# Attention's PSUM banks lent to the activation's u in steps 8 to 21, and VectorE's operations reordered there

## The chip, the core and the metric

The kernel runs on one core of one Trainium2 chip. The metric is the device time of one execution in microseconds (us). Five engines run side by side, each in its own program order, and wait for one another by semaphores: TensorE (PE in the rows; PEld is its weight load), VectorE (DVE), ScalarE (ACT), GpSimd (POOL) and SyncE (SP), which issues the DMAs. SBUF is the working memory. PSUM holds eight banks of 512 float32 words in each of 128 partitions; TensorE writes its products there.

## What is computed

A retention layer without softmax, and a feed-forward layer with a rational activation on its output:

```python
scores = scale * np.matmul(q, k.transpose(0, 1, 3, 2))      # q, k, v: 8 x 8 x 576 x 64
ret = scores * Dmat[None, :, :, :]                          # gamma_h ** (i - j) for i >= j, else 0
attn = np.matmul(ret, v)
x = attn.transpose(0, 2, 1, 3).reshape(B * S, H * D)        # 4608 x 512
h = x @ w_in                                                # 512 x 2048
P = a[0] + a[1] * h + a[2] * h**2 + a[3] * h**3
Q = 1.0 + np.abs(b[0]) * np.abs(h) + np.abs(b[1]) * h**2
out = (P / (Q + 1e-06)) @ w_out                             # 2048 x 512
```

## The kernel before, in words

Tokens are taken in nine blocks (b) of 512, the 2048 hidden columns in 16 chunks (f) of 128. One step is one pair (b, f). The plan `steps` (line 384) begins with chunks 0 to 7 of block 0 (steps 0 to 7), then has all 16 chunks of block 1 (steps 8 to 23), then chunks 8 to 15 of block 0 (steps 24 to 31), then blocks 2 to 8. 144 steps in all.

Every factor of a product is split in a high and a low part, and three products stand for one. `gemm1` (L282) makes h of a step with 12 matmuls of 512 columns into one of two PSUM banks (`ps_h`); `gemm2` (L347) adds the finished g of an earlier step to the block's sums with 12 more (four banks, `ps_acc`). Two banks (`ps_at`) belong to attention. That is all of PSUM.

Between the two lies the activation, on tiles u, v, p of 128 x 512 float32 in SBUF (u and v in two buffers, p in three):

- `ffn_p` (L293): ScalarE p = a3\*h + a2, then u = |h|; VectorE p = p\*h.
- `ffn_p2` (L303): VectorE p = (p + a1)\*h, the last reader of h.
- `ffn_v` (L307): ScalarE v = |b1|\*u + |b0|; VectorE v = v\*u.
- `ffn_r` (L313), one step later: ScalarE u = Ln(v), then u = Exp(-u), which is the reciprocal of the denominator.
- `ffn_q` (L319), one step later: VectorE p = (p + a0)\*u, v = (v + QC)\*u, p = (v - 2)\*p. The prediction calls these q1, q2, q3.
- `ffn_hi` (L335) and `ffn_lo` (L339), two steps later: ScalarE g's high part from p, then g's low part, on GpSimd for the first 24 steps and on VectorE after.

The weights arrive as 64-bit floats in 64-bit words and are taken apart on the way, one weight tile a step in steps 5 to 23, in `split_weight` (L139), a generator that `split_start` begins and `split_step(j)` moves on: `start` has ScalarE's copy of c, `split0`, `split1` and `split2` one VectorE operation each on c (split1 and split2 also read the words), `split3` ScalarE's high part of w and GpSimd's low part. The tile that one step starts gets its split0 in that step and split1 to split3 in the next.

Attention is done in units of 128 tokens, `scores` to `keep_lo`, in steps that `SCORES` (L50) lists: 1, 3 and 5, then 23, 25 and so on. In steps 8 to 21 none is at work; the scores of a unit are read for the last time in the step after.

The order of the work on each engine is the order in which the names stand in a list: `FIRST` (L34) for steps 0 to 23, `DENSE` and `REST` for later ones; `run` (L411) calls them in that order and leaves out those with nothing to do. `lag` (L387) says how many steps `gemm2` comes after `gemm1`: 4 in steps 8 to 21, otherwise 3 in this part, so step 22 runs two. After each step SP issues up to two loads of weights (`load_weights`). In steps 8 to 21 `FIRST` gives VectorE this order, with i the step:

```
split1, p*h (i), split2, p2 (i), split0, q1, q2, q3 (i-1), v*u (i)
```

The engine operations are all recorded at line 63, the wrapper that keeps program order, so the rows are told apart by their tiles: c<-bits is split1 or split2, TENSOR_SCALAR c<-c is split0, w<-c is split3.

Of the kernel before, what the change touches and what calls it, by code (L numbers as in the profile page):

```python
# [12 lines left out]
F32 = mybir.dt.float32  # L13
# [8 lines left out]
P = 128  # L22
# [7 lines left out]
NF = DFF // P  # L30
# [2 lines left out]
BEFORE = "split1 start scale_q scale_v scores decay outputs split2 add fade keep_hi keep_lo split3 split0".split()  # L33
FIRST = (  # L34
    "split1 gemm1 outputs ffn_p split2 ffn_hi keep_hi ffn_lo gemm2 ffn_r scale_q split3 add fade keep_lo start ffn_p2"
    " scale_v scores decay split0 ffn_q ffn_v"
).split()
DENSE = (
    "gemm1 outputs keep_hi split1 add fade keep_lo ffn_p split2 split0 ffn_v scale_q ffn_hi ffn_r ffn_lo scale_v gemm2"
    " ffn_p2 scores decay split3 ffn_q"  # L40
).split()
REST = (
    "gemm1 ffn_p outputs keep_hi add fade keep_lo ffn_hi ffn_p2 ffn_lo scores decay scale_q scale_v ffn_v gemm2 ffn_r ffn_q"
).split()
END = "ffn_r ffn_hi gemm2 ffn_lo ffn_q".split()

STARTS_BEFORE = [0, 1, 1, 2, 2]
STARTS = [1, 1, 2, 1, 2] + [1] * 19
# [1 line left out]
SCORES = [1, 3, 5, 23, 25, 27, 29, *range(2 * NF, (NB - 1) * NF, 4)]  # L50
# [16 lines left out]
def retention_ffn(ctx: ExitStack, tc: tile.TileContext, qkv, w_in, w_out, ab, masks, gq, gv, out):  # L67
# [20 lines left out]
    ps_at = ctx.enter_context(tc.tile_pool(name="ps_at", bufs=1, space=PSUM))  # L88
# [187 lines left out]
    els = {}  # L276
    gs = {}
    accs = {}
    part = []
    spare = {}  # L280

# [11 lines left out]
    def ffn_p(b, f):  # L293

        h = hs[b, f]
        u, v, p = els[b, f] = [
            (el3 if t == "p" else el).tile([P, 512], F32, tag=t, name=f"{t}{b}_{f}") for t in "uvp"
        ]
        act.activation(p, h, AF.Identity, bias=a2, scale=a3)
        act.activation(u, h, AF.Abs)  # L300
        dve.tensor_tensor(p, p, h, ALU.mult)
# [2 lines left out]
        p = els[b, f][2]  # L304
        dve.scalar_tensor_tensor(p, p, a1, hs.pop((b, f)), ALU.add, ALU.mult)

    def ffn_v(b, f):  # L307

        u, v, p = els[b, f]
        act.activation(v, u, AF.Identity, bias=b0, scale=b1)  # L310
        dve.tensor_tensor(v, v, u, ALU.mult)

    def ffn_r(b, f):  # L313
# [5 lines left out]
    def ffn_q(b, f):  # L319

        u, v, p = els[b, f]
        dve.scalar_tensor_tensor(p, p, a0, u, ALU.add, ALU.mult)
        dve.scalar_tensor_tensor(v, v, QC, u, ALU.add, ALU.mult)
        dve.scalar_tensor_tensor(p, v, 2.0, p, ALU.subtract, ALU.mult)

    def place(b, f):
# [54 lines left out]
    half = NF // 2  # L381
    first = half + NF
    runs = [(0, 0, half), (1, 0, NF), (0, half, NF)] + [(b, 0, NF) for b in range(2, NB)]
    steps = [(b, f, f == r0, f == r1 - 1) for b, r0, r1 in runs for f in range(r0, r1)]
    at = {s[:2]: i for i, s in enumerate(steps)}

    def lag(i):  # L387

        return 4 if NF // 2 <= i < first - 2 or i >= len(steps) - 8 else 3
# [6 lines left out]
    def load_weights(n):  # L396
        for k in [k for _, k in zip(range(n), loads)]:
            load_weight(k)
# [12 lines left out]
    def run(names, todo):  # L411
        todo |= {f"split{j}": (split_step, j) for j in range(4)}
        for name in names:
            if name in todo:
                todo[name][0](*todo[name][1:])
# [43 lines left out]
    for i in range(len(steps) + lag(len(steps))):  # L459
        this, prev, prev2 = (steps[j][:2] if 0 <= j < len(steps) else None for j in (i, i - 1, i - 2))  # L460
        todo = {"gemm2": (products, i), "start": (split_start, STARTS[i] if i < first else 0)}

        out_n = None
        if due and this:
            out_n = due.pop()
            todo |= {f.__name__: (f, out_n) for f in (keep_hi, add, keep_lo, fade)}
            todo["outputs"] = (put_out, out_n)
        if i in SCORES:
            todo |= {f.__name__: (f, nxt) for f in (scores, decay)}
            due.append(nxt)  # L470
            nxt += 1
        if i + 1 in SCORES:
            todo |= {f.__name__: (f, nxt) for f in (scale_q, scale_v)}
        if this:
            todo |= {f.__name__: (f, *this) for f in (gemm1, ffn_p, ffn_p2, ffn_v)}
        if prev:
            todo |= {f.__name__: (f, *prev) for f in (ffn_r, ffn_q)}
        if prev2:
            todo |= {"ffn_hi": (ffn_hi, *prev2), "ffn_lo": (ffn_lo, *prev2, i - 2 < first)}
        run(END if not this else FIRST if i < first else DENSE if i < 2 * NF else REST, todo)  # L480
        load_weights(2)


# [39 lines left out]
```

## Time and profile before

| | before |
|---|---|
| median of 3 runs | 989.28 us (988.65 to 990.79) |
| the profiled execution | 987.99 us, span 986.2 us |
| TensorE busy | 929.7 us, 94% |
| VectorE busy | 829.3 us, 84% |
| ScalarE busy | 708.0 us, 72% |
| GpSimd busy | 146.1 us, 15% |
| mean granted TensorE clock | 0.985 |
| HBM read, written | 54.93 MB, 9.44 MB |

The span goes from the first to the last instruction of one profiled execution. Busy is the time in which an engine had an instruction under way; an instruction that has started and stands still counts as busy. Matmuls overlap one another, so that their starts tell more than their lengths. A row of the timeline gives start, length, engine, line, operation, the tile written and the tiles read, the count, and in brackets the idle time before it with what ended that. GpSimd's spans are rough.

### The profile page before, as it was taken

Reading aid. Unit: us, or ns where it says so; the run is one execution under the profiler, and the core shown is the slowest. Engines: PE = TensorE matmul, PEld = TensorE weight load, DVE = VectorE, ACT = ScalarE, POOL = GpSimd, SP = SyncE. Lnnn points to the kernel's source line nnn. Section 1 sums busy time; section 2 is a strip of 40 time slices with the busy share of each in tenths; the row PEclk is TensorE's granted clock in tenths of the full one; section 3 lists DMA queues with packets and bytes.
Section 4 is the critical chain, followed back from the end, with each engine's and each line's share of the span. In section 5 each row is a group of like instructions: output and inputs, shape, how many; then the busy total and the mean of one; then the engine's idle time right before and its main releaser. Section 6 shows DMA issues by size and latency. Waiting matters only on the chain.

```text
span 986.2 us, 14758 instructions
## 1 busy us (share of the span) xinstructions
PE 929.7 (94%) x5658; PEld 752.2 (76%) x5658; DVE 829.3 (84%) x1189; ACT 708.0 (72%) x1274; POOL 146.1 (15%) x128
## 2 busy tenths in 40 slices
PE   7769878779999999999999999999999999999998
PEld 6557666567787888788888888888888888888886
DVE  3899989998789888888888887888788888888895
ACT  5577777778676777777777777777777777777775
POOL 3445333442100000000000000100000000000000
PEclk8799999999999999999999999999999999999999
DMA  9945000003212111210021112110211121001001
GB/s 346 407 160 213 1 0 1 1 0 109 91 59 86 44 44 41 71 56 22 32 81 44 44 44 86 44 65 22 86 44 44 43 86 44 1 1 44 1 1 43
DMA packets 20550, 65.31 MB, mean 66 GB/s; under 512 B 2304, under 2 KB 2432, under 8 KB 20480
## 3 DMA queue, kind: packets, MB, share of 16 engines
q1 hardware_dynamic: 20480, 64.37, 17.9%
q8 instruction: 44, 0.72, 0.3%
q14 instruction: 26, 0.21, 0.1%
HBM read 54.93 MB, written 9.44 MB: 65 GB/s over the span
## 4 chain that ended last, share of the span: by engine, by line
PE 71%; DVE 19%; ACT 5%; issue 3%; DMA 1%; SPq 0%; ACTq 0%; DVEq 0%
PE acc L63 32%; PE h L63 31%; PE ps L63 8%; DVE c L63 8%; DVE p L63 7%; DVE v L63 2%; ACT c L63 1%; ACT u L63 1%; DMA kv<-in_qkv 1%; ACT kv L63 1%; ACT v L63 1%; DVE s L63 1%; ACT o L63 1%; DMA qk<-in_qkv 0%; DVE xlo L63 0%
## 5 line engine op out<-in xcount | busy, mean ns | idle before, releaser
L63 PE MATMUL acc<-w,g 128*128 128x512 f32 x1632 | 402.3, 396 | 5.1 <-ACT o L63 4.0
L63 PE MATMUL h<-xhi,w 128*128 128x512 f32 x1152 | 381.9, 393 | 18.5 <-DVE p L63 17.3
L63 PEld LDWEIGHTS acc<-w,g 128*128 128x128 f32 x1632 | 303.3, 189 | 76.4 <-ACT o L63 4.8
L63 PEld LDWEIGHTS h<-xhi,w 128*128 128x128 f32 x1152 | 216.8, 188 | 70.0 <-DVE p L63 22.7
L63 PE MATMUL h<-xlo,w 128*128 128x512 f32 x576 | 225.1, 391 | 0.2 <-DVE xlo L63 0.2
L63 ACT ACTIVATE p<-h,ab_sb 128x512 f32<-128x512 f32 x144 | 111.4, 773 | 138.7 <-PE h L63 131.5
L63 DVE TENSOR_TENSOR p<-p,h 128x512 f32<-128x512 f32 x144 | 98.9, 687 | 44.3 <-ACT u L63 44.0
L63 DVE SCALAR_TENSOR_TENSOR p<-p,ab_sb,u 128x512 f32<-128x512 f32 x144 | 108.9, 756 | 27.0 <-ACT u L63 26.3
L63 ACT ACTIVATE u<-h 128x512 f32<-128x512 f32 x144 | 85.6, 595 | 60.0 <-DVE v L63 58.5
L63 PEld LDWEIGHTS h<-xlo,w 128*128 128x128 f32 x576 | 108.4, 188 | 22.5 <-DVE xlo L63 0.5
L63 DVE TENSOR_TENSOR v<-v,u 128x512 f32<-128x512 f32 x144 | 99.5, 691 | 27.8 <-ACT v L63 27.7
L63 ACT ACTIVATE v<-u,absb 128x512 f32<-128x512 f32 x144 | 116.3, 808 | 1.4 <-DVE p L63 1.1
L63 DVE SCALAR_TENSOR_TENSOR p<-p,ab_sb,h 128x512 f32<-128x512 f32 x144 | 107.1, 744 | 3.1
L63 ACT ACTIVATE u<-u,lnb 128x512 f32<-128x512 f32 x144 | 104.5, 725 | 4.7
L63 POOL TENSOR_TENSOR S_sb<-S_sb,gv_sb 128x256 f32<-128x256 f32 x32 | 20.4, 638 | 575.8 <-DVE S_sb L63 572.6
L63 DVE SCALAR_TENSOR_TENSOR p<-v,p 128x512 f32<-128x512 f32 x144 | 100.6, 699 | 5.0
L63 ACT ACTIVATE u<-v,lnb 128x512 f32<-128x512 f32 x144 | 103.3, 718 | 0.2 <-DVE v L63 0.2
L63 DVE SCALAR_TENSOR_TENSOR v<-v,u 128x512 f32<-128x512 f32 x144 | 99.4, 691 | 0.0
L63 DVE TENSOR_TENSOR g<-p,g 128x512 fp32r<-128x512 f32 x112 | 90.2, 805 | 1.4 <-ACT g L63 1.4
L63 ACT ACTIVATE g<-p 128x512 fp32r<-128x512 f32 x136 | 85.7, 630 | 6.9 <-DVE p L63 3.3
L63 ACT ACTIVATE kv<-kv,gv_sb 128x64 f32<-128x64 f32 x288 | 72.6, 341 | 10.0 <-DMA gv_sb<-in_gv 6.3
L63 DVE SCALAR_TENSOR_TENSOR c<-bits,c 128x512 int32<-128x512 int32 x64 | 57.8, 914 | 0.1
(35 smaller groups left out, 623.7 us busy)
## 6 DMA issues: line engine op xcount, KB each, us to landing
qk<-in_qkv SPq DMA_DIRECT2D x36, 512.0 KB, 4.8
kv<-in_qkv SPq DMA_DIRECT2D x36, 512.0 KB, 3.9
bits<-in_w_in SPq DMA_DIRECT2D x16, 512.0 KB, 10.2
bits<-in_w_out SPq DMA_DIRECT2D x16, 512.0 KB, 10.2
out<-o SPq DMA_DIRECT2D x16, 512.0 KB, 3.2
out<-o SPq DMA_DIRECT2D x4, 256.0 KB, 2.3
gq_sb<-in_gq SPq DMA_DIRECT2D x1, 256.0 KB, 2.7
mask_sb<-in_masks SPq DMA_DIRECT2D x1, 128.0 KB, 6.3
```

Of the source, the lines that this page charges most:

```text
L63: return lambda *a, **k: self.tc.keep_in_program_order(method(*a, **k))
```

## The change

In steps 8 to 21 the list `MID` sets the order. At step 8 one tile of attention's two PSUM banks is taken, and u of these steps lies in its half f % 2; at step 22 it is given up. `ffn_v` is cut into its ScalarE part `ffn_va` and its VectorE part, `ffn_q` into its first two operations and `ffn_q3`. The other lists name the new pieces right behind the old ones.

```diff
 FIRST = (
...
-    " scale_v scores decay split0 ffn_q ffn_v"
+    " scale_v scores decay split0 ffn_q ffn_q3 ffn_va ffn_v"
+).split()
+MID = (
+    "split1 split2 gemm1 ffn_p ffn_hi ffn_lo gemm2 ffn_p2 ffn_r split3 ffn_q ffn_va ffn_v ffn_q3 start split0"
 ).split()
...
-END = "ffn_r ffn_hi gemm2 ffn_lo ffn_q".split()
+END = "ffn_r ffn_hi gemm2 ffn_lo ffn_q ffn_q3".split()
...
+    free_at = []
...
         u, v, p = els[b, f] = [
+            free_at[f % 2] if t == "u" and free_at else
             (el3 if t == "p" else el).tile([P, 512], F32, tag=t, name=f"{t}{b}_{f}") for t in "uvp"
         ]
...
-    def ffn_v(b, f):
+    def ffn_va(b, f):
 
         u, v, p = els[b, f]
         act.activation(v, u, AF.Identity, bias=b0, scale=b1)
+
+    def ffn_v(b, f):
+        u, v, p = els[b, f]
         dve.tensor_tensor(v, v, u, ALU.mult)
...
         dve.scalar_tensor_tensor(p, p, a0, u, ALU.add, ALU.mult)
         dve.scalar_tensor_tensor(v, v, QC, u, ALU.add, ALU.mult)
+
+    def ffn_q3(b, f):
+        u, v, p = els[b, f]
         dve.scalar_tensor_tensor(p, v, 2.0, p, ALU.subtract, ALU.mult)
...
-        run(END if not this else FIRST if i < first else DENSE if i < 2 * NF else REST, todo)
+        if i == half:
+            ps = ps_at.tile([P, 2, 512], F32, tag="at", name="free_at")
+            free_at.extend((ps[:, 0], ps[:, 1]))
+        elif i == SCORES[3] - 1:
+            free_at.clear()
+        run(END if not this else MID if free_at else FIRST if i < first else DENSE if i < 2 * NF else REST, todo)
```

`DENSE` and `REST` change as `FIRST` does. In steps 8 to 21 VectorE's order is then

```
split1, split2, p*h (i), p2 (i), q1, q2 (i-1), v*u (i), q3 (i-1), split0
```

and ScalarE's p (i), u (i), g's high part (i-2), Ln, Exp (i-1), w's high part, v (i), c; before, it was the same but for c, which stood ahead of v.

## Rows read from the trace of the kernel before

**Rows 1.** Busy time by stretches: length, engines' busy us (instructions), PEclk, DMA share, GB/s.
```profile
core 0: us, PE busy (x) PEld busy (x) DVE busy (x) ACT busy (x) POOL busy (x), PEclk, DMA share, GB/s
103.30:197.90 94.60, 76.17 (x312) 58.66 (x312) 85.66 (x117) 69.36 (x107) 36.83 (x26) 0.98 0.00 1
...
400.00:600.00 200.00, 198.91 (x1236) 161.68 (x1235) 167.15 (x245) 145.40 (x265) 13.13 (x14) 1.00 0.15 53
```

**Rows 2.** Waits from 103 to 198 us: total us, times, longest.
```profile
PE h L63 <- DVE p L63: 17.3, 12, 1.5
...
ACT u L63 <- DVE v L63: 14.1, 13, 1.1
```

**Rows 3.** Timeline of VectorE, one step and the next one's split1.
```profile
137.09 0.68 DVE L63 SCALAR_TENSOR_TENSOR c<-bits,c 128x512 int32<-128x512 int32 x1
137.69 0.68 DVE L63 TENSOR_TENSOR p<-p,h 128x512 f32<-128x512 f32 x1
138.29 1.19 DVE L63 SCALAR_TENSOR_TENSOR c<-bits,c 128x512 int32<-128x512 int32 x1
139.40 0.73 DVE L63 SCALAR_TENSOR_TENSOR p<-p,ab_sb,h 128x512 f32<-128x512 f32 x1
140.74 1.06 DVE L63 TENSOR_SCALAR c<-c 128x512 int32<-128x512 int32 x1 [0.60 <-ACT c L63]
141.72 0.74 DVE L63 SCALAR_TENSOR_TENSOR p<-p,ab_sb,u 128x512 f32<-128x512 f32 x1
142.39 0.68 DVE L63 SCALAR_TENSOR_TENSOR v<-v,u 128x512 f32<-128x512 f32 x1
143.10 0.69 DVE L63 SCALAR_TENSOR_TENSOR p<-v,p 128x512 f32<-128x512 f32 x1
143.71 0.69 DVE L63 TENSOR_TENSOR v<-v,u 128x512 f32<-128x512 f32 x1
144.31 0.68 DVE L63 SCALAR_TENSOR_TENSOR c<-bits,c 128x512 int32<-128x512 int32 x1
```

**Rows 4.** Timeline of GpSimd over the same step.
```profile
137.37 1.56 POOL L63 TENSOR_TENSOR g<-p,g 128x512 fp32r<-128x512 f32 x1 [3.07 <-issue]
140.22 1.29 POOL L63 TENSOR_TENSOR w<-c,w 128x512 fp32r<-128x512 f32 x1 [1.29 <-ACT w L63]
144.59 1.56 POOL L63 TENSOR_TENSOR g<-p,g 128x512 fp32r<-128x512 f32 x1 [3.07 <-issue]
```

**Rows 5.** Timeline of ScalarE over the same step, four of its operations.
```profile
139.51 0.63 ACT L63 ACTIVATE w<-c 128x512 fp32r<-128x512 f32 x1 [0.82 <-DVE c L63]
...
140.61 0.80 ACT L63 ACTIVATE v<-u,absb 128x512 f32<-128x512 f32 x1
...
143.16 0.60 ACT L63 ACTIVATE u<-h 128x512 f32<-128x512 f32 x1 [1.08 <-DVE v L63]
143.82 0.63 ACT L63 ACTIVATE g<-p 128x512 fp32r<-128x512 f32 x1
```

**Rows 6.** Instructions on tile c, whole span: shortest/median/longest ns, first and last start.
```profile
L63 DVE TENSOR_SCALAR c<-c x32: 412/1070/1520, 18.5 to 220.9; 128x512 int32<-128x512 int32 x32
```

**Rows 7.** Timeline of VectorE: split1 of step 8 and of step 22.
```profile
107.38 0.68 DVE L63 SCALAR_TENSOR_TENSOR c<-bits,c 128x512 int32<-128x512 int32 x1
...
209.27 0.68 DVE L63 SCALAR_TENSOR_TENSOR c<-bits,c 128x512 int32<-128x512 int32 x1
```

**Rows 8.** Timeline of VectorE: split0 in the step that stores partial sums.
```profile
133.53 1.05 DVE L63 TENSOR_SCALAR c<-c 128x512 int32<-128x512 int32 x1 [1.42 <-ACT c L63]
```

**Rows 9.** Timeline of VectorE and GpSimd in step 2, which splits two weight tiles.
```profile
65.01 2.36 DVE L63 SCALAR_TENSOR_TENSOR c<-bits,c 128x512 int32<-128x512 int32 x2
...
65.23 1.59 POOL L63 TENSOR_TENSOR g<-p,g 128x512 fp32r<-128x512 f32 x1 [3.02 <-ACT g L63]
...
67.89 1.28 DVE L63 SCALAR_TENSOR_TENSOR c<-bits,c 128x512 int32<-128x512 int32 x2
```

**Rows 10.** Timeline of TensorE: first matmul of two consecutive steps with no wait.
```profile
134.64 0.39 PE L63 MATMUL h<-xhi,w 128*128 128x512 f32 x1
...
140.19 0.50 PE L63 MATMUL h<-xhi,w 128*128 128x512 f32 x1
```

More of the change, by code (lines that the diff above doesn't have):

```diff
@@ L35 @@
     "split1 gemm1 outputs ffn_p split2 ffn_hi keep_hi ffn_lo gemm2 ffn_r scale_q split3 add fade keep_lo start ffn_p2"
-    " scale_v scores decay split0 ffn_q ffn_v"
+    " scale_v scores decay split0 ffn_q ffn_q3 ffn_va ffn_v"
+).split()
+MID = (
+    "split1 split2 gemm1 ffn_p ffn_hi ffn_lo gemm2 ffn_p2 ffn_r split3 ffn_q ffn_va ffn_v ffn_q3 start split0"
 ).split()
 DENSE = (
-    "gemm1 outputs keep_hi split1 add fade keep_lo ffn_p split2 split0 ffn_v scale_q ffn_hi ffn_r ffn_lo scale_v gemm2"
-    " ffn_p2 scores decay split3 ffn_q"
+    "gemm1 outputs keep_hi split1 add fade keep_lo ffn_p split2 split0 ffn_va ffn_v scale_q ffn_hi ffn_r ffn_lo scale_v gemm2"
+    " ffn_p2 scores decay split3 ffn_q ffn_q3"
 ).split()
 REST = (
-    "gemm1 ffn_p outputs keep_hi add fade keep_lo ffn_hi ffn_p2 ffn_lo scores decay scale_q scale_v ffn_v gemm2 ffn_r ffn_q"
+    "gemm1 ffn_p outputs keep_hi add fade keep_lo ffn_hi ffn_p2 ffn_lo scores decay scale_q scale_v ffn_va ffn_v gemm2 ffn_r ffn_q ffn_q3"
 ).split()
-END = "ffn_r ffn_hi gemm2 ffn_lo ffn_q".split()
+END = "ffn_r ffn_hi gemm2 ffn_lo ffn_q ffn_q3".split()
 STARTS_BEFORE = [0, 1, 1, 2, 2]
@@ L305, in ffn_p2 @@
         dve.scalar_tensor_tensor(p, p, a1, hs.pop((b, f)), ALU.add, ALU.mult)
+    def ffn_va(b, f):
+        u, v, p = els[b, f]
+        act.activation(v, u, AF.Identity, bias=b0, scale=b1)
     def ffn_v(b, f):
         u, v, p = els[b, f]
-        act.activation(v, u, AF.Identity, bias=b0, scale=b1)
         dve.tensor_tensor(v, v, u, ALU.mult)
@@ L474, in retention_ffn @@
         if this:
-            todo |= {f.__name__: (f, *this) for f in (gemm1, ffn_p, ffn_p2, ffn_v)}
+            todo |= {f.__name__: (f, *this) for f in (gemm1, ffn_p, ffn_p2, ffn_va, ffn_v)}
         if prev:
-            todo |= {f.__name__: (f, *prev) for f in (ffn_r, ffn_q)}
+            todo |= {f.__name__: (f, *prev) for f in (ffn_r, ffn_q, ffn_q3)}
         if prev2:
             todo |= {"ffn_hi": (ffn_hi, *prev2), "ffn_lo": (ffn_lo, *prev2, i - 2 < first)}
-        run(END if not this else FIRST if i < first else DENSE if i < 2 * NF else REST, todo)
+        if i == half:
[4 more added lines that the diff above has]
+        run(END if not this else MID if free_at else FIRST if i < first else DENSE if i < 2 * NF else REST, todo)
         load_weights(2)
```

## The prediction

> **What bounds the kernel now.** I read the busy time by stretches first [rows 1]. From 400 to 600 us TensorE is busy 198.91 of 200 us: nothing can be won there except by less work. Steps 8 to 21 of the plan lie in the first stretch, where TensorE leaves 18 of 94.6 us unused, VectorE (DVE) is busy 85.66 us, DMA is still and the granted clock is 0.98, the upper of its levels. The waits say who holds TensorE up there: its first matmul of a step waits for DVE's p, 12 times, 17.3 us together [rows 2]. That p is ffn_p2, the last reader of h, and h has two buffers.
>
> So DVE's own timeline is next [rows 3]. One step lasts 144.31 - 137.09 = 7.22 us, and all of it is DVE: nine operations back to back and one gap of 0.60 us, where split0 waits for ScalarE's copy of c. Seven of the nine take 0.68 to 0.74 us. Two are longer than their kind: split2 takes 1.19 us where split1, the same form, takes 0.68; split0 takes 1.06 us where its shortest is 0.412 [rows 6]. Both lie over a GpSimd operation [rows 4]: g's low part runs until 137.37 + 1.56 = 138.93, and split2 ends 0.55 us later; w's low part runs until 141.51, and split0 ends 0.29 us later. The p\*h between them, at 137.69, also lies under GpSimd and takes its usual 0.68: it reads one operand from PSUM. So in this trace a DVE operation whose tensors are all in SBUF stands still while GpSimd reads SBUF, and one with a PSUM input doesn't.
>
> **The change, part by part.** No instruction is added or removed: a step keeps 9 DVE, 8 ScalarE and 2 GpSimd operations, 24 matmuls and the weight loads that SP issues at its end; only the order on each engine and the place of u change. The lists of the other steps name the same instructions in the same order, since each new name stands right behind the one it was cut from. So the sum is: 14 steps, old length against new.
>
> *Old.* split1 of step 8 starts at 107.38 and split1 of step 22 at 209.27 [rows 7]: 101.89 us, or 13 steps of 7.22 and one of 8.0. In that one ScalarE also stores the first block's partial sums, and split0 waits 1.42 us [rows 8].
>
> *u in PSUM.* Three more operations (both with u in ffn_q, and v\*u) become PSUM readers. The trace has the same forms on h: ffn_p2, with a scalar and PSUM, 0.73 against 0.74 for ffn_q's first on SBUF; p\*h 0.68 against 0.69 for v\*u [rows 3]. I take no difference. Bounds: 0.06 us less, or 0.06 us more (the spread of the forms there), that is up to 2.5 us of 14 times 3 operations either way. [...]
>
> ScalarE's four operations on u lose their wait for a buffer (14.1 us in the stretch, [rows 2]). A PSUM destination is not in the trace; the nearest rows are a plain operation from PSUM, 0.60 (u<-h), and one from SBUF, 0.63 (g) [rows 5]. I bound each by three times that difference, 0.1 us either way, and cost it at nothing. Its cover: ScalarE is busy 69.36 us in 94.6, 5.3 us a step of 7.22.
>
> *The new DVE order* is split1, split2, p\*h, p2, q1, q2, v\*u, q3, split0. Two operations that don't depend on each other start 0.60 us apart, a dependent one some 0.03 after the end of the one before (q2 to q3: 0.71), q1 to q2 0.67 [rows 3]. What GpSimd meets decides the rest. g's high part starts on ScalarE 0.03 us after q3 ends (143.79), and g's low part on GpSimd 0.80 us after q3's end, at 144.59 [rows 4, 5]. With q3's end as zero, split0 now runs from -0.09 to 0.32 and split1 from 0.36 to 1.04: GpSimd asks in the middle of split1, and split2 stands behind it. That is a pattern the trace has [rows 9]: two c operations in a row took 1.28 us when alone, but 2.36 us when g's low part started 0.22 us into the first. GpSimd waited for the first to end (65.69), ran until 66.82, 1.13 us later, and the second ended 0.55 us after that. So I take it that the waiting GpSimd goes first. Then, from split1's start: split1 ends 0.68, GpSimd 1.81, split2 2.36; p\*h starts 2.28, p2 3.00, q1 3.66, q2 4.33, v\*u 4.93, q3 5.53, split0 6.13, the next split1 at 6.13 + 0.41 + 0.04 = 6.58.
>
> *What has to be ready by then.* w's high part waits for split2 and can start at about 2.4; it and v<-u take 0.63 and 0.80 [rows 5], so v is there by 3.9, before v\*u at 4.93. w's low part runs on GpSimd from about 3.1 to 4.4 (1.29 us, [rows 4]), all under PSUM readers; so split0 is short. The copy of c stands right behind v<-u and has until 6.13: the 0.60 gap is gone. u<-h needs the bank that q2 frees at 5.0 and ends at 5.7, before q3's end at 6.2. TensorE's 24 matmuls take 140.19 - 134.64 = 5.55 us when nothing holds them [rows 10], so it still waits for p2, about 1.0 us a step.
>
> *Sum.* 14 times 6.58 = 92.1 us, and 0.2 for the step with the stores, which now delays v\*u a little: 92.3 instead of 101.9, a gain of 9.6 us. It carries to the end: behind step 22 DVE's order is the old one, everything it does comes 9.6 us earlier, and TensorE, held by DVE until the next attention unit is through, follows it. The PSUM tile is free when step 8 takes it (the unit of step 5 is read in step 6), and step 23's scores, which need it back, come behind two whole steps of matmuls, after q2 of step 21. The profiled execution took 987.99 us, so 978.4; the median of the runs is 1.29 above it: **979.7 us**. With the PSUM bounds this case spans 977 to 983.
>
> **Rivals.**
> *No meeting.* If g's low part asked 0.3 us later, behind split2's start, or if split2 went first, it would run under p\*h and p2, and DVE's step would be 6.58 - 0.96 = 5.62 us, level with TensorE's 5.55. 14 times 5.62 is 78.7, the gain 23.0 us, the time 966.3. For it: 0.3 us is little, and a later ScalarE would bring it about. Against: u<-h ends half a microsecond before q3 does, so g starts with q3's end in every step; and who goes first is what [rows 9] show. If only some steps escape, the time lies between 966 and 978.
>
> *A second meeting, slower.* If ScalarE ran 1.2 us later in its step (w's high part ends near 4.3 instead of 3.0), w's low part would still be reading when q3 asks at 5.53, and q3 would wait up to another 1.1 us. A step of 7.6 us makes 106.4 us for the stage, 4.5 more than now: 993.8. That takes an extra 0.3 us on each of the four ScalarE operations on u, three times my bound; but the bound is an estimate, and q3 is a pure SBUF operation right behind the five, so it is where a late GpSimd lands.
>
> *No gain.* If each of the three operations on u cost 0.21 us more from PSUM, the 0.64 us a step are gone and the time stays at 989.3. The rows of the two kinds [rows 3] allow a third of that at most.
>
> **How the numbers follow.** Chances: the forecast 0.60; no meeting or only in part 0.21; small gain or none by dearer PSUM operations 0.08; second meeting 0.11. The range takes in the first two and part of the third: 964.5 to 984, about 0.82. A measurement of this kernel can tell 0.2%, some 2 us, from no change. Faster by more: 0.60 + 0.21 + 0.02 = 0.83; within: 0.06; slower: 0.11.
>
> **What would show it.** Right: in steps 8 to 21 of the new trace DVE steps of 6.5 to 6.6 us without a gap, split2 at about 1.7 us with g's low part over it, split0 at 0.41, the five PSUM operations at 0.68 to 0.74, TensorE's wait for p at some 1.0 us a step, split1 of step 22 near 199.7. If split2 takes 0.68 and the step 5.6, the first rival holds; if q3 takes over 1 us, the second; if the three operations on u are longer than 0.8, the third. What lies behind step 24 should be shifted and otherwise the same; if it is longer there, the sum missed a cost of the hand-over.

## The result and the profile after

The changed kernel takes 991.96 us, median of 10 runs (991.17 to 993.44), the kernel before 988.6 us on the same chips (986.04 to 990.79): 1.0034 times, 95% interval 1.0023 to 1.0044. Faster by 9.6 us was forecast; it is slower by 3.4.

The busy time by stretches, same columns as [rows 1] (line 66 is the wrapper of line 63, moved down by three lines; the tile free_at is u of steps 8 to 21):

```profile
core 0: us, PE busy (x) PEld busy (x) DVE busy (x) ACT busy (x) POOL busy (x), PEclk, DMA share, GB/s
103.30:197.90 94.60, 76.45 (x302) 58.52 (x301) 84.03 (x113) 62.32 (x101) 31.45 (x25) 0.95 0.00 1
...
400.00:600.00 200.00, 198.91 (x1236) 161.67 (x1235) 167.11 (x244) 147.00 (x267) 12.92 (x15) 1.00 0.15 50
```

From 400 to 600 us nothing has changed. In the stage itself (steps 8 to 21) all engines got through fewer instructions in the same time, VectorE 113 where it had 117, ScalarE 101 where it had 107. VectorE's timeline has the stage's two ends, to be read against [rows 7] (c<-bits x2 is split1 and split2, which now follow each other):

```profile
106.56 2.43 DVE L66 SCALAR_TENSOR_TENSOR c<-bits,c 128x512 int32<-128x512 int32 x2
...
213.41 0.69 DVE L66 SCALAR_TENSOR_TENSOR c<-bits,c 128x512 int32<-128x512 int32 x1
```

The 14 steps take 106.85 us, 4.96 more than before; the stage began 0.82 us earlier in this execution, so step 22 begins 4.14 later, and the span is 4.3 us longer. The whole difference is made in the stage, and the forecast of 92.3 us for it is 14.5 short. One step of VectorE, to be read against [rows 3]:

```profile
144.29 2.53 DVE L66 SCALAR_TENSOR_TENSOR c<-bits,c 128x512 int32<-128x512 int32 x2
146.75 0.68 DVE L66 TENSOR_TENSOR p<-p,h 128x512 f32<-128x512 f32 x1
147.46 0.75 DVE L66 SCALAR_TENSOR_TENSOR p<-p,ab_sb,h 128x512 f32<-128x512 f32 x1
148.12 0.74 DVE L66 SCALAR_TENSOR_TENSOR p<-p,ab_sb,free_at 128x512 f32<-128x512 f32 x1
148.78 0.68 DVE L66 SCALAR_TENSOR_TENSOR v<-v,free_at 128x512 f32<-128x512 f32 x1
150.31 0.69 DVE L66 TENSOR_TENSOR v<-v,free_at 128x512 f32<-128x512 f32 x1 [0.85 <-ACT v L66]
150.91 0.68 DVE L66 SCALAR_TENSOR_TENSOR p<-v,p 128x512 f32<-128x512 f32 x1
151.51 0.42 DVE L66 TENSOR_SCALAR c<-c 128x512 int32<-128x512 int32 x1
151.97 2.53 DVE L66 SCALAR_TENSOR_TENSOR c<-bits,c 128x512 int32<-128x512 int32 x2
```

Much is as forecast: split0 has fallen from 1.06 to 0.42 us, its gap of 0.60 is gone, the five PSUM readers take 0.68 to 0.75 us, and split2 stands behind GpSimd (the pair takes 2.53 us where two alone take 1.28, [rows 9]). But there is a new gap: v\*u waits 0.85 us for ScalarE's v. It starts 1.53 us after q2 in place of 0.60, and the step is 7.68 us long. ScalarE and GpSimd beside it, against [rows 4, 5]:

```profile
144.98 1.30 POOL L66 TENSOR_TENSOR g<-p,g 128x512 fp32r<-128x512 f32 x1 [3.82 <-issue]
...
147.56 1.28 POOL L66 TENSOR_TENSOR w<-c,w 128x512 fp32r<-128x512 f32 x1 [1.29 <-ACT w L66]
...
149.50 0.78 ACT L66 ACTIVATE v<-free_at,absb 128x512 f32<-128x512 f32 x1 [2.01 <-DVE v L66]
```

v<-u, behind w's high part, had nothing left to wait for by the data: its u and its buffer of v were ready. It stood still for 2.01 us and began 0.04 us after q2's end (148.78 + 0.68 = 149.46). q2 belongs to the step before and reads the other half of the PSUM tile. The waits from 107 to 200 us show it as a new pair; of the three lines only the second has a counterpart in [rows 2]:

```profile
ACT v L66 <- DVE v L66: 21.1, 11, 2.0
...
PE h L66 <- DVE p L66: 17.5, 11, 2.2
...
DVE v L66 <- ACT v L66: 9.3, 11, 0.9
```

The lines are in the order of the answer: ScalarE's v for VectorE, TensorE's h for VectorE's p (17.3 before), VectorE's v\*u for ScalarE. Step 8 is the exception that points to the cause. Its q1 and q2 belong to step 7, whose u is still in SBUF, and there v waits for nothing (q2 begins only at 111.48, after v); the u of step 9, though, which goes into the other bank, waits for step 8's v\*u (112.09 + 0.67 = 112.76):

```profile
109.56 0.76 ACT L66 ACTIVATE v<-free_at,absb 128x512 f32<-128x512 f32 x1
...
112.79 0.58 ACT L66 ACTIVATE free_at<-h 128x512 f32<-128x512 f32 x1 [1.24 <-DVE v L66]
```

### The profile page after: what moved, and what is told of

The parts are those of the page before. It is cut to its first block, busy times and chain, and to the rows that moved or that the text cites. A ratio compares the mean times of both kernels' runs of the same rounds, so it can differ in the third digit from the quotient of the medians.

```text
span 990.5 us, 14756 instructions
## 1 busy us (share of the span) xinstructions
PE 932.0 (94%) x5658; PEld 753.6 (76%) x5658; DVE 831.6 (84%) x1189; ACT 703.6 (71%) x1274; POOL 142.4 (14%) x128
## 4 chain that ended last, share of the span: by engine, by line
PE 70%; DVE 17%; DMA 5%; ACT 4%; issue 4%; SPq 0%; ACTq 0%; DVEq 0%
PE acc L66 32%; PE h L66 30%; PE ps L66 8%; DVE p L66 8%; DVE c L66 5%; DVE v L66 3%; DMA bits<-in_w_in 3%; ACT v L66 1%; DMA bits<-in_w_out 1%; ACT u L66 1%; DMA qk<-in_qkv 1%; ACT o L66 1%; DVE s L66 1%; ACT kv L66 1%; ACT g L66 0%
## 5 line engine op out<-in xcount | busy, mean ns | idle before, releaser
L66 DVE SCALAR_TENSOR_TENSOR p<-p,ab_sb,u 128x512 f32<-128x512 f32 x130 | 99.0, 762 | 26.9 <-ACT u L66 26.2
L66 DVE TENSOR_TENSOR v<-v,u 128x512 f32<-128x512 f32 x130 | 89.9, 691 | 27.8 <-ACT v L66 27.7
L66 ACT ACTIVATE u<-h 128x512 f32<-128x512 f32 x130 | 77.2, 594 | 43.7 <-DVE v L66 42.2
L66 ACT ACTIVATE v<-u,absb 128x512 f32<-128x512 f32 x130 | 105.0, 808 | 1.3 <-DVE p L66 1.1
L66 ACT ACTIVATE u<-u,lnb 128x512 f32<-128x512 f32 x130 | 94.3, 725 | 4.2
L66 ACT ACTIVATE u<-v,lnb 128x512 f32<-128x512 f32 x130 | 93.1, 716 | 0.2 <-DVE v L66 0.2
L66 DVE SCALAR_TENSOR_TENSOR v<-v,u 128x512 f32<-128x512 f32 x130 | 89.9, 692 | 0.0
L66 DVE SCALAR_TENSOR_TENSOR c<-bits,c 128x512 int32<-128x512 int32 x64 | 66.5, 1048 | 1.0
```

The source lines that it names most:

```text
L66: return lambda *a, **k: self.tc.keep_in_program_order(method(*a, **k))
```

## The experiments

Theory A: the two banks are the two halves of one tile, and operations of different engines on one PSUM tile are put in the order in which the program names them, even two readers, even of different banks. `ffn_q` is named ahead of `ffn_va`, so v waits for q2. Theory B: the two engines hold each other up when they read PSUM at the same time. A third question ran along, whether GpSimd's meeting with split2 costs what the prediction took.

**Two tiles in place of two halves.** Attention's pool of PSUM is closed at step 8, a pool with two one-bank tiles is opened, and closed again ahead of step 23. Each ratio from here on is to the kernel before on the same chip.

```diff
-            free_at[f % 2] if t == "u" and free_at else
+            free_at[0].tile([P, 512], F32, tag="fu", name=f"fu{b}_{f}") if t == "u" and free_at else
...
-            ps = ps_at.tile([P, 2, 512], F32, tag="at", name="free_at")
-            free_at.extend((ps[:, 0], ps[:, 1]))
+            banks.close()
+            free_at.append(banks.enter_context(tc.tile_pool(name="ps_u", bufs=2, space=PSUM)))
```

> The changed kernel, but u of even and odd steps lies in two PSUM tiles of one bank each, in place of the two halves of one tile; every engine's order is unchanged. Theory A (one tile: ScalarE's v of step i is made to wait for q2 of step i-1 because both read the same tile): the wait of 2.01 us before v and the 0.85 us before v*u go, a step shrinks from 7.68 to about 6.75 us, 14 steps by 13 us, time about 979. Theory B (ScalarE and VectorE hold each other up when they read PSUM at the same time, whatever the tiles): the wait stays, time about 992. Both expect split2 to stand behind g's low part as in the changed kernel (split1 and split2 together 2.5 us).

Measured: 978.19 us, 0.9904 of before (0.9889 to 0.9919). One step of VectorE, with ScalarE's v and GpSimd:

```profile
140.08 2.39 DVE L66 SCALAR_TENSOR_TENSOR c<-bits,c 128x512 int32<-128x512 int32 x2
...
140.50 1.42 POOL L66 TENSOR_TENSOR g<-p,g 128x512 fp32r<-128x512 f32 x1 [2.61 <-issue]
...
143.04 0.76 ACT L66 ACTIVATE v<-fu,absb 128x512 f32<-128x512 f32 x1
...
145.02 0.68 DVE L66 TENSOR_TENSOR v<-v,fu 128x512 f32<-128x512 f32 x1
...
146.68 2.39 DVE L66 SCALAR_TENSOR_TENSOR c<-bits,c 128x512 int32<-128x512 int32 x2
```

The tile fu is u. v waits for nothing and is ready 1.2 us before v\*u is due. The step is 6.60 us, the prediction's sum said 6.58. Theory B falls: the banks that attention gave up, read by the same engines in the same order, and no wait; v takes its 0.76 us although VectorE's p2 reads PSUM at the same time (from 143.10).

**One tile, another order of naming.** Only the list changes; each engine's order stays.

```diff
-    "... ffn_r split3 ffn_q ffn_va ffn_v ffn_q3 start split0"
+    "... ffn_r split3 ffn_va ffn_q ffn_v ffn_q3 start split0"
```

> The changed kernel with one tile as it is; only the place of ffn_va in the list changes, it is written down ahead of ffn_q. Each engine still has the same order. Theory A: now q1 of step i-1 is the later reader of the tile and waits for v, which ends about when q1 is due anyway (v ends some 3.9 us after split1's start, q1 is due at 3.85), so a step takes 6.8 to 6.9 us and the time is about 980. Theory B: nothing that the engines do changes, 992.

Measured: 979.88 us, 0.9923 (0.9906 to 0.9939); the step is 6.67 us. v no longer waits, and q1 now begins 0.04 us behind v's end and 0.73 after p2's start, where the changed kernel has 0.66, as theory A has it:

```profile
143.88 0.76 ACT L66 ACTIVATE v<-free_at,absb 128x512 f32<-128x512 f32 x1
...
144.68 0.75 DVE L66 SCALAR_TENSOR_TENSOR p<-p,ab_sb,free_at 128x512 f32<-128x512 f32 x1
```

So the wait is not in the data and not in the memory: it was put into the program, and the place of a name in a list decides which operation waits.

**g later, two tiles.** g's high and low part come behind Ln and Exp, so that GpSimd asks later.

```diff
-    "split1 split2 gemm1 ffn_p ffn_hi ffn_lo gemm2 ffn_p2 ffn_r split3 ..."
+    "split1 split2 gemm1 ffn_p gemm2 ffn_p2 ffn_r ffn_hi ffn_lo split3 ..."
```

> Two tiles, and g's high part (ScalarE) and low part (GpSimd) come after Ln and Exp in place of before them, so that GpSimd asks while split2 runs and gets its turn under p*h and p2. If the meeting of g's low part with split2 costs what the prediction took, split1 and split2 together fall from 2.5 to about 1.4 us, a step to 5.6 to 5.8 us, TensorE's 5.55 us become the bound, time about 966. If split2 waits for another reason, the step stays near 6.75 us and the time near 979.

Measured: 967.02 us, 0.9784 (0.9769 to 0.9798), the fastest of all and ahead of both kernels. VectorE and GpSimd in one step, and then the busy time from 150 to 190 us:

```profile
143.37 1.42 DVE L66 SCALAR_TENSOR_TENSOR c<-bits,c 128x512 int32<-128x512 int32 x2
...
144.49 1.46 POOL L66 TENSOR_TENSOR g<-p,g 128x512 fp32r<-128x512 f32 x1 [2.92 <-issue]
144.71 0.68 DVE L66 TENSOR_TENSOR p<-p,h 128x512 f32<-128x512 f32 x1
...
145.91 1.30 POOL L66 TENSOR_TENSOR w<-c,w 128x512 fp32r<-128x512 f32 x1
...
149.00 0.69 DVE L66 SCALAR_TENSOR_TENSOR c<-bits,c 128x512 int32<-128x512 int32 x1
```

```profile
150.00:190.00 40.00, 40.00 (x173) 31.75 (x172) 39.31 (x65) 34.96 (x56) 20.15 (x15) 1.00 0.00 0
```

GpSimd now comes while split2 runs, waits until it ends (144.79), as far as its length tells (1.46 us, w's low part 1.30), and does both its operations under the five PSUM readers. The step is 5.63 us, and TensorE has no idle time left (40.00 of 40.00): the stage has changed its bound. This is the rival "no meeting" with its 5.62 us and 966.3, brought about by the order.

**The order alone.** u stays in SBUF; free_at is left as a flag that selects `MID`.

```diff
-            free_at[f % 2] if t == "u" and free_at else
```

> The new order with u in SBUF as before, so without the PSUM tile. Theory A: no wait of v for q2; but q1 now has only SBUF tensors and stands behind w's low part, which runs from 3.3 to 4.55 us after split1's start: q1 takes about 1.3 instead of 0.74 us, a step 7.3 us, time about 987. Theory B: no PSUM readers to hold each other up, the same 987; it differs from A in the first two runs. If the new order itself were what makes v late, v would wait here too, and a step would take 8 us or more, time over 996.

Measured: 989.24 us, 1.0008 (0.9997 to 1.002), a step of 7.14 us. q1 is now an SBUF operation under w's low part and takes 1.27 us, ending when GpSimd has (147.41) and 0.55 more:

```profile
146.13 1.28 POOL L66 TENSOR_TENSOR w<-c,w 128x512 fp32r<-128x512 f32 x1 [1.29 <-ACT w L66]
...
146.69 1.27 DVE L66 SCALAR_TENSOR_TENSOR p<-p,ab_sb,u 128x512 f32<-128x512 f32 x1
```

Against the two-tile run the place of u is worth 7.14 - 6.60 = 0.54 us a step, all of it the meeting that q1 is spared (0.74 us there). That is 7.7 us in the stage (100.63 against 92.97); the rest of the 11 us between the two runs lies behind the stage, where this run lost 3.7 us against the kernel before (last section). So the order alone does gain 1.3 us in its stage; its time doesn't show it.

**The place alone.** Two tiles, but `FIRST` for every step up to 23.

```diff
-        run(END if not this else MID if free_at else FIRST if i < first else DENSE if i < 2 * NF else REST, todo)
+        run(END if not this else FIRST if i < first else DENSE if i < 2 * NF else REST, todo)
```

> u of steps 8 to 21 in two PSUM tiles, but in the order of the kernel before. GpSimd's two operations then still meet split2 and split0, which are SBUF operations in either place, and the five PSUM readers don't stand where GpSimd is at work. If the place of u matters only through what GpSimd meets, a step stays at 7.2 us and the time at 987 to 989. If reading u from PSUM were cheaper or dearer by itself, it shows here: 0.06 us on each of three operations would be 2.5 us.

Measured: 987.75 us, 0.9985 (0.9975 to 0.9996); a step of 7.20 us against 7.22. Reading u from PSUM was not dearer on VectorE in this run; if anything the step gains 0.02.

**One tile, g later; and the same with ffn_va first.** The edits of above, put together on the changed kernel.

> The changed kernel with its one tile, and only g's two parts moved behind Ln and Exp. If the two costs found so far are apart (the meeting of g's low part with split2, and v's wait for q2), the first goes and the second stays: a step of 5.63 + 0.95 = 6.6 us, time 977, between the two-tile runs. If v's wait vanishes as well once ScalarE's order changes, it falls to about 967.

> As the run before it, with ffn_va also written down ahead of ffn_q. Theory A: q1 now waits for v, and u of the next step for v*u, through the one tile; these two waits close a loop of v*u, u, Ln, Exp, g, w, v, q1, q2 of about 5.8 us, so a step takes 5.8 us and the time is 968 to 970, 2 us behind the two-tile run with g late. If one tile costs nothing once the list is written so, 967; if v still waits for q2, 977.

Measured: 979.1 us (0.99, 0.9882 to 0.9917) and 969.3 us (0.9806, 0.9789 to 0.9824), steps of 6.57 and 5.75 us. In the first the wait for q2 is back, and with it the gap before v\*u; in the second v waits for nothing, and q1 starts 0.03 us behind v's end (146.82 + 0.77 = 147.59, q1 at 147.62). The rows are of the first:

```profile
144.44 0.78 ACT L66 ACTIVATE v<-free_at,absb 128x512 f32<-128x512 f32 x1 [1.59 <-DVE v L66]
...
145.25 0.69 DVE L66 TENSOR_TENSOR v<-v,free_at 128x512 f32<-128x512 f32 x1 [0.85 <-ACT v L66]
```

The four runs make a square: early g 992.0 with the wait and 978.2 without, late g 979.1 and 967.0. In the same order the stages, from split1 of step 8 to that of step 22, are 106.85, 92.97, 93.42 and 81.20 us long. By the stages the wait costs 13.9 and 12.2 us, the meeting 13.4 and 11.8: two costs that nearly add up, neither a form of the other.

**g later, u in SBUF.** The order-alone kernel with g late.

> The new order with g late and u in SBUF: the PSUM tile alone taken away from the fastest run. split2 is free of GpSimd as there, but w's low part runs right behind g's, from about 2.6 to 3.8 us after split1's start, and q1, due at 2.7, now has SBUF tensors only: it waits some 0.9 us. A step of 6.5 us, time about 978. If the order alone makes the gain, 967; if GpSimd's meeting with q1 also delays v and what hangs on it, above 980.

Measured: 979.77 us, 0.9907 (0.9888 to 0.9926), a step of 6.54 us. q1 stands behind w's low part:

```profile
143.51 1.29 POOL L66 TENSOR_TENSOR w<-c,w 128x512 fp32r<-128x512 f32 x1
...
143.69 1.66 DVE L66 SCALAR_TENSOR_TENSOR p<-p,ab_sb,u 128x512 f32<-128x512 f32 x1
```

So in the fastest run PSUM is worth 6.54 - 5.63 = 0.91 us a step, and the idea of the change holds.

**One SBUF tile with two halves.** The order-alone kernel, u in the halves of one tile for the whole span.

```diff
+    uu = elu.tile([P, 2, 512], F32, name="uu")
...
+            uu[:, f % 2] if t == "u" else (el3 if t == "p"
```

> The new order with u in SBUF, as in the order-alone run (989.2 us), but u of even and odd steps in the two halves of one SBUF tile. If any two readers of one tile are put in order, v of step i waits for q2 of step i-1 here too, a step takes 8 us in place of 7.13 and the time is above 1000. If that holds for tiles in PSUM alone, v waits for nothing, and the time is 987 to 991.

Measured: 989.1 us, 1.0006 (0.9989 to 1.0023), like separate buffers. v waits for nothing: its row has no bracket, and q2 of the step before begins 1.94 us after it. So the order among readers was kept for the PSUM tile and not for this SBUF tile.

```profile
145.26 0.80 ACT L66 ACTIVATE v<-uu,absb 128x512 f32<-128x512 f32 x1
...
147.20 0.68 DVE L66 SCALAR_TENSOR_TENSOR v<-v,uu 128x512 f32<-128x512 f32 x1
```

## Why the prediction was wrong, by its own steps

*What bounds the kernel* held: VectorE's step set TensorE's waits before and after, and where the step fell to 5.63 us TensorE filled up.

*u in PSUM* held for the cost of the operations, on both engines. The trace's rows on the tile free_at have q1 at 743 ns, q2 at 680, v\*u at 689, like their SBUF rows in [rows 3]. The place-alone run agrees, with a step of 7.20 us against 7.22. ScalarE came out a little cheaper (shortest, median, longest ns):

```profile
L66 ACT ACTIVATE free_at<-v,lnb x14: 672/686/705, 113.9 to 213.8; 128x512 f32<-128x512 f32 x14
L66 ACT ACTIVATE free_at<-free_at,lnb x14: 662/662/663, 114.6 to 214.6; 128x512 f32<-128x512 f32 x14
```

Before, in the same stage, Ln and Exp took 726 and 725 on average; the bound of 0.1 us either way contained it. One sentence of this part put a gain in the wrong place: it is not by the place that u's operations lose their wait for a buffer, since two banks are no more than two buffers. The place-alone run still has it, 11.5 us from 103 to 198 us (14.1 in [rows 2]); the two-tile run with the new order has none. The sum had priced it at nothing.

*The new DVE order* held. GpSimd goes first when it asks during split1, and split2 pays; the two-tile run has the sum's 6.58 us as 6.60, and its stage is 92.97 us long where 92.3 were summed.

*What has to be ready by then* is the step that failed: "so v is there by 3.9, before v\*u at 4.93". It went through the data that each operation needs and the buffers it overwrites, and v lacked none of these. It left out the wait that was put into this program for two operations on one PSUM tile (2.01 us in the step shown above), that is, it gave this overlap of ScalarE's v with VectorE's q1 and q2 no cost. With it, v comes after q2: 149.50 - 144.29 = 5.2 after split1's start instead of some 3.0. This makes 0.93 us of the 1.10 by which a step is longer than forecast. The rest is a consequence: late v makes ScalarE's next steps late, GpSimd's g asks 0.69 us after split1's start in place of 0.42 (two tiles), split2 is held longer, and p\*h starts 2.46 us after split1 where 2.28 was summed. 13 such steps give 14.1 us; step 8 adds 0.6, because its q1 still reads u in SBUF and meets w's low part (it takes 1.27 us), which the sum also overlooked; less the 0.2 summed for the stores, which no step shows, that is the 14.5 missing in the stage.

The *rivals* had the sign of the outcome at 0.11, by a mechanism that did not occur (q3 takes 0.68 us, no second meeting). Both two-tile times, 978.19 and 967.02 us, lie inside the forecast's range.

The hand-over behind step 21 cost nothing, as forecast: step 22 begins 4.14 us later and the span ends 4.3 us later.

## What to carry to other kernels

When buffers are laid into one PSUM tile, look in the trace for an operation that starts 0.04 us behind another engine's operation on the other half: give each buffer a tile of its own (12 to 14 us here), or name the early reader first, which took back 12.1 of 13.8 and 9.8 of 12.1 us. In these runs a VectorE operation with a PSUM input took its usual time while GpSimd was at work (over w's low part q1 took 0.74 us with u in PSUM, 1.27 with u in SBUF); what that is worth depends on when GpSimd asks, so its producer on ScalarE has to be placed as carefully as VectorE's order. And in a blind sum, ask of every moved instruction not only what it needs but what the framework will order it behind.

## What the runs showed of the hardware that was not expected

In the changed kernel a GpSimd operation that started right at the end of a VectorE operation on SBUF still went ahead of the next one: g's low part started 0.69 us after split1, whose kind takes 0.68, and the pair still took 2.53 us. Two such operations start 0.60 us apart when alone (1.28 for both, [rows 9]), so the first rival's condition, "behind split2's start", was not enough. With g late and two tiles GpSimd started 1.12 us after split1 and waited; no run has a start between the two.

TensorE's granted clock in the stage was 0.95, against 0.98 before [rows 1] (a mean: 1.00 from 103 to 129 us, 0.50 from 131 to 133, 1.00 from 135 to 200), and 1.00 from 150 to 190 us of the fastest run. In the changed kernel, after a wait of 1.94 us, the matmuls of one step began to start 0.43 us apart in place of 0.23. From 155.9 to 160 us the granted clock was 0.65, a mean over two levels: from 150 to 157 us it was 1.00, from 157.5 to 160.5 us 0.50, from 161 to 163 us 1.00 again.

```profile
150.66 0.39 PE L66 MATMUL h<-xlo,w 128*128 128x512 f32 x1
150.89 0.39 PE L66 MATMUL h<-xhi,w 128*128 128x512 f32 x1
...
155.93 0.50 PE L66 MATMUL h<-xhi,w 128*128 128x512 f32 x1 [1.94 <-DVE p L66]
...
158.16 0.63 PE L66 MATMUL h<-xlo,w 128*128 128x512 f32 x1
158.59 1.05 PE L66 MATMUL h<-xhi,w 128*128 128x512 f32 x2
```

There it cost nothing that the rows show: VectorE's step was 7.68 us like its neighbours, since TensorE waited for p in these steps anyway.

Behind the stage it did cost time. From split1 of step 22 to the end the kernel before takes 986.2 - 209.27 = 776.9 us, the order-alone run 987.9 - 207.31 = 780.6. Its granted clock fell there twice, to 0.59 and 0.63 in the stretches below, and the same 12 matmuls into acc took 4.34 and 4.62 us where they take 3.02 and 3.01 in the kernel before. First the kernel before, then the order-alone run:

```profile
222.74 3.02 PE L63 MATMUL acc<-w,g 128*128 128x512 f32 x12
...
244.75 3.01 PE L63 MATMUL acc<-w,g 128*128 128x512 f32 x12 [1.79 <-ACT o L63]
```

```profile
207.31 0.69 DVE L66 SCALAR_TENSOR_TENSOR c<-bits,c 128x512 int32<-128x512 int32 x1
...
222.11 4.34 PE L66 MATMUL acc<-w,g 128*128 128x512 f32 x12
...
244.89 4.62 PE L66 MATMUL acc<-w,g 128*128 128x512 f32 x12 [1.80 <-ACT o L66]
```

```profile
244.89:249.51 4.62, 4.62 (x14) 3.37 (x14) 2.36 (x4) 4.55 (x8) 0.00 (x0) 0.63 0.59 227
219.15:226.29 7.14, 7.14 (x45) 5.63 (x45) 7.11 (x11) 4.01 (x8) 2.31 (x3) 0.59 0.45 148
```

The run with one SBUF tile lost 3.8 us behind the stage, g late with u in SBUF 2.7, one tile with g late 1.5; in the other runs this part is within 0.3 us of the kernel before. So some times of the experiments are longer than their steps alone would make them. Why the granted clock fell in the order-alone run is not shown: the kernel before has the same waits of TensorE ahead of both places (3.35 us and 1.79 us), and its granted clock there stayed at 1.00.
